# Sixteen more fulfilled semaphore instructions in ScalarE's stream, behind its first small loads

## The chip, the cores and the metric

The kernel runs on one core of a Trainium2 chip. The metric is the device time of one execution in microseconds (us); lower is better. The core has five engines with a queue of instructions each: TensorE (PE, whose weight loads are shown as PEld), VectorE (DVE), ScalarE (ACT), GpSimd (POOL) and SyncE (SP). They run on their own and wait for each other through semaphores, which are counters: a producer adds to one when it is done, and a consumer waits until it has reached a value.

## The reference

The kernel mixes a state-space branch and a dense branch with a gate. The input `x` has 2048 rows (time steps) of 640 columns, in bf16.

```python
x = A_x
g = _sigmoid((x * gate_w).sum(-1, keepdims=True))
# a: complex diagonal state-space model
dt = jnp.exp(log_dt)
Lam_bar = jnp.exp(dt * Lam)
B_bar = ((Lam_bar - 1.0) / Lam)[:, None] * Bmat
Bu = jnp.einsum("bld,pd->blp", x + 0j, B_bar)
for t in range(L):
    h = Lam_bar[None, :] * h + Bu[:, t, :]
y = 2.0 * jnp.einsum("blp,dp->bld", hseq, Cmat).real + x * Dskip[None, None, :]
# b: gelu MLP, hidden width 1728
h = jnp.einsum("bsd,df->bsf", x, w1) + b1
h = _gelu(h)
b = jnp.einsum("bsf,fd->bsd", h, w2) + b2
return g * a + (1 - g) * b
```

## The kernel before, in words

The 2048 time steps are cut into four quarters of 512 (`q`), and the recurrence into eight blocks of 256 (`ssm(b)`). For each quarter TensorE does five kinds of work: the hidden layer of the dense branch (`m1`, x times w1, L653 for its first eight column groups and L675 for the rest), the input projection of the state-space branch (`bproj`, L718), the second layer (`mains` in `outsT` and the like, L1013 and L807), the output projection (L1083, L920), and small tails. Each group of matmuls fills one of eight PSUM banks, and ScalarE empties it: gelu for `m1` (L662 for the first eight groups, L682 for the rest), a copy for `bproj` (L727). VectorE computes tables from the small vectors once, and then multiplies, scans and combines.

The order on each engine is not written out by hand. Each operation is added with `op(name, eng, dur, reads, writes, fn, prio)`. A planner (`Sched.order`) runs through time and takes, on each engine, the operation with the lowest `prio` number among those whose predecessors are finished by its own estimates. What then comes out is one fixed stream for each engine. `Emitter.wait` (its `wait_ge` stands on L139) writes the waits ahead of an operation, one for each semaphore that the engine has not yet waited for to that value. The build step then places such waits on instructions: a wait either sits on the instruction itself or on an EVENT_SEMAPHORE instruction of its own in the same queue.

The start of the kernel is where the change lies:

- GpSimd sets the tile `rows` to zero (`rz`, L386) and increments `pool_s`, the first value of that semaphore.
- ScalarE issues six DMAs: one piece of w1 (`w1load(0, "act", -110, reads=["rz"])`), which waits for `rz`, and then the small vectors into rows of `rows`: b1b (priority -101), `lre`, `lim`, `ldt` and `b1a` (-100 to -97).
- TensorE warms up (L416), transposes pieces of x (L428), and starts the hidden layer (L653). In between it transposes `rows` (L455), and VectorE copies the result to `cols` (L460, operation `cols1`).
- ScalarE takes the exponential of a part of `cols` (`dt`, L465), and VectorE and ScalarE in turn make angles (L470, L471, L485 to L493), a magnitude (`amag`, L478) and two sines (L498, L499), from which VectorE makes the tables of the state-space branch.
- Then ScalarE does the gelus of the first eight groups (L662), in the order of the banks 0 to 7. The ninth group of matmuls, the first of L675, takes bank 0 over again and so waits for the first gelu.

Exp, Sin and gelu need different function tables in ScalarE. The build step puts an ACT_TABLE_LOAD into ScalarE's stream wherever the next function is not in the table that is loaded; there are three, shown with the lines 465, 498 and 662 of the operations that need them.

The first operations of that chain are

```python
        def f_dt():
            return inc("act", nc.scalar.activation(dtb[:, :], lcol[:, 2, :], ACT.Exp))

        op("dt", "act", 0.3, ["lcol"], ["dtb"], f_dt, prio=-950)
```

`lcol` is a part of `cols`. The number -950 puts `dt` ahead of everything else on ScalarE as soon as `cols` is there in the planner's time, and not before.

Of the kernel before, what the change touches and what calls it, by code (L numbers as in the profile page):

```python
# [147 lines left out]
class Prog:  # L148
# [8 lines left out]
    def op(self, name, eng, dur, reads, writes, fn, prio=None, lat=0.0, after=()):  # L157
        deps = {}
        for k in reads:
            for w in self.last_w.get(k, ()):  # L160
                deps[w.idx] = w
        for k in writes:
            for w in self.last_w.get(k, ()):
                deps[w.idx] = w
            for r in self.last_r.get(k, ()):
                deps[r.idx] = r
        for a in after:
            deps[a.idx] = a
        deps = list(deps.values())
        E = self.E  # L170

        def run(eg, deps=deps, eng=eng, fn=fn):
            E.wait(eng, *[d.done for d in deps if not (eng == "pe" and d.eng == "pe")])
            return fn()

        it = self.sch.add(name, eng, dur, deps, run, prio=prio, lat=lat)
        for k in writes:
            self.last_w[k] = [it]
            self.last_r[k] = []
        for k in reads:  # L180
            self.last_r.setdefault(k, []).append(it)
        return it


def bass_gated_mix__ssm_conv_s5__dense_activation_gelu__prompt_kernel(
# [18 lines left out]
    _, S, D = A_x.shape  # L204
# [21 lines left out]
    with ExitStack() as es:  # L226
# [69 lines left out]
        sems = {}  # L296
# [11 lines left out]
        op = pr.op  # L308
# [108 lines left out]
            return inc("pe", t)  # L417

        op("warm", "pe", 2.7, (), [("bank", 4)], f_warm, prio=-1000)

        for i, (k, c0, c1) in enumerate(((0, 0, 2), (1, 0, 2), (0, 2, 4), (1, 2, 4))):
            bank = (7, 6, 7, 6)[i]
# [777 lines left out]
```

## Time and profile before

| What | us |
|---|---|
| median of the three runs | 212.67 (212.52 to 212.89) |
| profiled execution, first to last instruction (span) | 211.0 |
| difference, time around the span | 1.6 to 1.7 |
| PE busy | 207.5 (98%) |
| DVE busy | 191.1 (91%) |
| ACT busy | 102.7 (49%) |
| POOL busy | 4.2 (2%) |

The profile is of one execution, and of that it gives the span; the time around it is what the median of the other runs has beyond the span. Busy times leave out instructions that only wait or issue. The mean granted clock of TensorE is 1.000 over the span. An engine's share of the span is a mean over stages; what counts at a place in time is who waits for whom there. The profile has these views: the chain that ended last, followed back from the last instruction; a timeline of instructions, with the idle time before each and what ended it; and, for a source line, all instructions of that line, semaphore instructions among them, which the timeline leaves out. Times in all views are counted from the first instruction. Names such as "ACTq" or "PEldq" mean the queue of that engine.

### The profile page before, as it was taken

To read this page: it belongs to the slowest core of one execution; us is meant where nothing else is said; L and a number is where in the kernel's file an instruction comes from. 1 tells how busy PE (TensorE), PEld (TensorE's weight loads), DVE (VectorE), ACT (ScalarE), POOL (GpSimd) and SP (SyncE) were. 2 spreads that over 40 slices of the span, in tenths; PEclk is the share of its full clock that TensorE was granted. 3 is DMA by queue.
4 is the path that set the end of the run, shared out by engine and by line. 5 is a ranking of instruction groups with operands and counts; after the bars stand their busy time and mean duration, and the time that the engine had idled before them with its cause. 6 is when DMAs were issued, how large, how long until landed. Compare 5 with 4: busy or idle time off the path is not lost.

```text
span 211.0 us, 2539 instructions
## 1 busy us (share of the span) xinstructions
PE 207.5 (98%) x987; PEld 95.7 (45%) x1004; DVE 191.1 (91%) x244; ACT 102.7 (49%) x166; POOL 4.2 (2%) x12
## 2 busy tenths in 40 slices
PE   8999999999999999999999999999999999999996
PEld 4544444444444444444444444444444444444444
DVE  2399999999999999999999999899999999899482
ACT  2399556678950523556674222456665243304321
POOL 1000000030000000000010000000010000000000
DMA  6999999999800020043464000005622000006623
GB/s 190 259 221 118 203 173 216 381 203 175 184 2 4 0 50 0 0 95 67 90 57 117 0 3 0 0 2 116 150 59 100 0 0 4 0 0 141 134 76 99
DMA packets 50247, 19.47 MB, mean 92 GB/s; under 512 B 43068, under 2 KB 48828, under 8 KB 50236
## 3 DMA queue, kind: packets, MB, share of 16 engines
q1 hardware_dynamic: 47904, 17.59, 39.5%
q0 software_dynamic: 1600, 1.32, 4.2%
q10 hardware_dynamic: 732, 0.40, 0.8%
q8 instruction: 8, 0.13, 0.3%
q14 instruction: 3, 0.02, 0.1%
HBM read 8.68 MB, written 2.63 MB: 54 GB/s over the span
## 4 chain that ended last, share of the span: by engine, by line
PE 98%; issue 0%; DVE 0%
PE ps L675 22%; PE ps L718 20%; PE ps L1013 20%; PE ps L1083 15%; PE ps L807 5%; PE ps L653 4%; PE ps L920 4%; PE ps L827 1%; PE ps L416 1%; PE ps L696 1%; PE ps L880 1%; PE ps L1048 1%; PE ps L428 0%; PE ps L844 0%; DVE W1sb L952 0%
## 5 line engine op out<-in xcount | busy, mean ns | idle before, releaser
L675 PE MATMUL ps<-xT,W1sb 128*128 128x512 bf16 x214 | 47.5, 379 | 0.3
L760 DVE TENSOR_TENSOR_SCAN W<-atab,V 128x1280 bf16<-128x1280 f32 x16 | 44.3, 2811 | 0.3
L718 PE MATMUL ps<-xT,BT 128*128 128x512 bf16 x196 | 43.3, 379 | 0.2
L1013 PE MATMUL ps<-Gl,W2sb 128*128 128x512 bf16 x192 | 42.8, 379 | 0.2
L682 ACT ACTIVATE Gl<-ps,cols 128x512 bf16<-128x512 f32 x44 | 29.9, 695 | 15.5 <-PE ps L675 15.5
L675 PEld LDWEIGHTS ps<-xT,W1sb 128*128 128x128 bf16 x220 | 21.5, 98 | 26.0
L1083 PE MATMUL ps<-Hb,CT 128*128 128x512 bf16 x150 | 32.9, 379 | 0.0
L727 ACT ACTIVATE U<-ps 128x512 bf16<-128x512 f32 x40 | 23.6, 596 | 14.7 <-PE ps L718 14.7
L718 PEld LDWEIGHTS ps<-xT,BT 128*128 128x128 bf16 x200 | 19.5, 98 | 23.8 <-ACT Gt L704 0.4
L1013 PEld LDWEIGHTS ps<-Gl,W2sb 128*128 128x128 bf16 x195 | 18.9, 98 | 23.3 <-issue 0.7
L1083 PEld LDWEIGHTS ps<-Hb,CT 128*128 128x128 bf16 x150 | 14.7, 98 | 17.7
L1021 ACT ACTIVATE E1T<-ps,cols 128x512 bf16<-128x512 f32 x15 | 10.0, 687 | 26.2 <-PE ps L1013 14.7
L1091 ACT ACTIVATE E2T<-ps 128x512 bf16<-128x512 f32 x15 | 9.0, 597 | 21.7 <-PE ps L1083 21.7
L627 DVE SCALAR_TENSOR_TENSOR trf<-xn,gwb 128x640 bf16<-128x640 bf16 x16 | 13.2, 823 | 0.4
L505 DVE TENSOR_TENSOR Hb<-Hb,V 128x1280 bf16<-128x1280 bf16 x16 | 12.5, 822 | 0.3
L505 DVE TENSOR_TENSOR V<-V,W 128x1280 bf16<-128x1280 bf16 x16 | 12.5, 821 | 0.3
L505 DVE TENSOR_TENSOR V<-mr,U 128x2560 bf16<-128x2560 bf16 x8 | 11.9, 1492 | 0.3
L505 DVE TENSOR_TENSOR Hb<-c,W 128x2560 bf16<-128x2560 bf16 x8 | 11.9, 1490 | 0.2
L807 PE MATMUL ps<-W2sb,Gl 128*128 128x512 bf16 x51 | 11.8, 379 | 0.1
L505 DVE TENSOR_TENSOR W<-mi,U 128x2560 bf16<-128x2560 bf16 x8 | 11.9, 1484 | 0.0
L505 DVE TENSOR_TENSOR V<-s,W 128x2560 bf16<-128x2560 bf16 x8 | 11.9, 1484 | 0.0
L1071 ACT ACTIVATE xT<-xT,cols 128x512 bf16<-128x512 bf16 x15 | 10.0, 713 | 0.9 <-DMA cols<-in_A_Dskip_dram 0.9
(103 smaller groups left out, 149.4 us busy)
## 6 DMA issues: line engine op xcount, KB each, us to landing
W2sb<-in_B_w_dram SPq DMA_DIRECT2D x1, 2080.0 KB, 8.7
out_dram<-xn SPq DMA_DIRECT2D x3, 640.0 KB, 5.7
xn<-in_A_x_dram POOLq DMA_DIRECT2D x2, 640.0 KB, 6.9
W1sb<-in_B_w_dram SPq DMA_DIRECT2D x4, 256.0 KB, 4.0
trf<-grow SPq DMA_DIRECT2D x4, 256.0 KB, 4.8
xn<-in_A_x_dram SPq DMA_DIRECT2D x1, 640.0 KB, 7.6
W1sb<-in_B_w_dram SPq DMA_DIRECT2D x1, 480.0 KB, 6.1
W1sb<-in_B_w_dram SPq DMA_DIRECT2D x1, 400.0 KB, 6.9
```

Source lines behind the costliest of these rows:

```text
L505: return inc("dve", nc.vector.tensor_tensor(out=o, in0=a, in1=b, op=o_))
L627: t = inc("dve", nc.vector.scalar_tensor_tensor(out=scr[:, :], in0=xn[q % 2][:, c, :], scalar=1.0, in1=gwb[:, :], op0=ALU.mult, op1=ALU.mu ...
L675: t = nc.tensor.matmul(PS[bank][:, :], W1sb[:, k, jf * 128:(jf + 1) * 128], xT[q][:, k, :], start=(k == 0), stop=(k == KD - 1))
L682: return inc("act", nc.scalar.activation(Gl[q % 2][:, jf, :], PS[bank][:, :], ACT.Gelu_apprx_tanh, bias=b1col[:, jf:jf + 1]))
L718: t = nc.tensor.matmul(PS[bank][:, :], BT[:, ci, kd, k * 128:(k + 1) * 128], xT[q][:, kd, :], start=(kd == 0), stop=(kd == KD - 1))
L727: return inc("act", nc.scalar.activation(dst, src, ACT.Copy, scale=1.0 if ci == 0 else -1.0))
L760: t = inc("dve", nc.vector.tensor_tensor_scan(out=g[:, ci, :], data0=a, data1=v[:, ci, :], initial=0.0, op0=ALU.mult, op1=ALU.add))
L807: t = nc.tensor.matmul(PS[bank][:, :], Gl[q % 2][:, jf, t4 * 128:(t4 + 1) * 128], W2sb[:, jf, 0:DN], start=False, stop=False, skip_group_c ...
L1013: t = nc.tensor.matmul(PS[bank][:, :], W2sb[:, jf, d * 128:(d + 1) * 128], Gl[q % 2][:, jf, :], start=(jf == 0 and not lead), stop=(jf == ...
L1021: return inc("act", nc.scalar.activation(E1T[:, d, :], PS[bank][:, :], ACT.Identity, bias=cols2[:, 0, d:d + 1]))
L1071: return inc("act", nc.scalar.activation(xT[q][:, d, :], xT[q][:, d, :], ACT.Copy, scale=cols2[:, 1, d:d + 1]))
L1083: t = nc.tensor.matmul(PS[bank][:, :].rearrange("p (s t) -> p s t", s=2), CT[:, ci, k, d * 128:(d + 1) * 128], Hb[:, 2 * (q % 2):2 * (q % ...
```

## The change

An operation `pad` is added for ScalarE. It has 32 calls of `wait_ge` on `pool_s` for the value 1, reads `rz` and writes nothing. Its priority is -96.

```diff
         op("warm", "pe", 2.7, (), [("bank", 4)], f_warm, prio=-1000)
 
+        def f_pad():
+            for _ in range(32):
+                nc.scalar.wait_ge(sems["pool_s"], 1)
+
+        op("pad", "act", 0.1, ["rz"], [], f_pad, prio=-96)
+
         for i, (k, c0, c1) in enumerate(((0, 0, 2), (1, 0, 2), (0, 2, 4), (1, 2, 4))):
```

In the built program this gives sixteen more semaphore instructions on ScalarE. What they ask of `pool_s` was already fulfilled when ScalarE's first DMA was issued.

## The prediction

> **What bounds the kernel now.** I read the chain of waits that ended last first, then the timeline of ScalarE around the place of the change, then the semaphore records there.
>
> ```profile
> PE 98%; issue 0%; DVE 0%
> ```
>
> TensorE is the chain for 98% of the span: whatever costs time must open a gap on PE. The chain cut to 12 to 20 us shows how PE passes from the first hidden-layer matmuls (L653, eight banks filled in turn) to the next ones (L675, which take the banks over again):
>
> ```profile
> 11.81 2.16 PE ps L653 x10
> 13.97 5.40 PE ps L675 x25
> ```
>
> There is no gap at that seam, and the chain nowhere passes through ACT. The timeline of ScalarE from 3 to 21 us is the view that decides here:
>
> ```profile
> 3.64 0.40 ACTq L333 DMA_DIRECT2D rows<-in_B_b_dram  x1
> 4.07 1.28 ACT L465 ACT_TABLE_LOAD   x1 [4.07 <-issue]
> 8.62 0.21 ACT L465 ACTIVATE dtb<-cols 128x5 bf16<-128x5 f32 x1 [3.27 <-DVE cols L460]
> 9.14 0.21 ACT L478 ACTIVATE amag<-acol 128x5 f32<-128x5 f32 x1 [0.31 <-DVE thcol L471]
> 9.36 1.28 ACT L498 ACT_TABLE_LOAD   x1
> 10.72 0.34 ACT L498 ACTIVATE trf<-trf 128x165 f32<-128x165 f32 x1
> 10.96 0.32 ACT L499 ACTIVATE trf<-trf 128x165 f32<-128x165 f32 x1
> 11.31 1.28 ACT L662 ACT_TABLE_LOAD   x1
> 12.60 4.74 ACT L662 ACTIVATE Gl<-ps,cols 128x512 bf16<-128x512 f32 x8
> ```
>
> Columns: start, duration, engine and line. ScalarE issues its last small load until 4.04, loads the table for Exp at once (4.07 to 5.35), and then waits 3.27 us for `cols` from VectorE (L460, ends at 8.59). The load of the table thus lies wholly inside a wait. From 8.62 on nothing is idle: Exp, Exp, a second table, two Sin, a third table, and at 12.60 the first gelu, which ends at 13.29 and frees the first bank.
>
> The last view is PE's own semaphore records between 13.2 and 13.5 us (L139 is the line of every wait):
>
> ```profile
> L139 PEldq EVENT_SEMAPHORE  x1: 51/51/51, 13.3 to 13.3; - x1
> ```
>
> By the trace's records it starts 0.04 us after the first gelu ends: TensorE's queue is already waiting for ScalarE there, and only work queued ahead (to 13.81, where the first L675 matmul starts) hides it. So ScalarE's chain from 8.62 is a second critical path, with a small slack.
>
> **That slack.** Gelu ends 13.29; +0.04 to the semaphore record; +0.05 for it; +0 to 0.10 until the weight load starts (the record that ends at 2.01 has one 0.003 us behind it; 0.10 is an assumed upper end); +0.005 to 0.054 from weight load to matmul (the rows at 3.98 and at 8.14). An unhindered start is 13.385 to 13.535, the real one 13.81: slack 0.28 to 0.42 us. I take 0.33.
>
> **The change, part by part.** Nothing is removed. `f_pad` asks 32 times for a value of `pool_s` that the w1 load at 0.97 has already waited for.
>
> *Place.* Priority -96 puts it behind the last of the small loads (-97) and ahead of the Exp of L465, which needs `cols`. Its planned 0.1 us ends long before the planner has `cols` ready, so no other engine's order should move, and it adds no increment and no DMA.
>
> *How waits become instructions.* The records show one wait on an ACTIVATE and up to two on a semaphore record ahead of it: the five waits in front of L455 are one on the transpose and two records with two each (7.2 to 7.4 us). They also show which goes where: the wait written first sits on the instruction itself (`l_lre` at L455), and the one written last stays on the semaphore record next to it. For L465 that makes 32 + 1 = 33 waits: one on the ACTIVATE, 32 on sixteen records. This is the sixteen of the title. But the wait on `cols` is the one written last, so it goes from the ACTIVATE to the sixteenth record, and a fulfilled one takes its place.
>
> *The sixteen as such.* No row shows such records back to back on ScalarE. One there lasts 17 ns; with pauses, two on SP (L1169) start 58 ns apart, two on PE (64.6 us) 111 ns. Fifteen cost 0.26 us (15 x 17 ns) to 1.7 us (15 x 111), by the SP rows 0.87. They run from 4.04 to at most 5.7, and 8.59 is when `cols` comes: hidden by VectorE's lateness on either bound, cost 0. Without that cover it would be 0.9 us.
>
> *What is queued behind the sixteenth.* It now holds ScalarE's queue until 8.59, and everything behind it: the first ACT_TABLE_LOAD, if that stands between the records and the ACTIVATE. The trace has no case of a table load with semaphore records ahead. The three loads there are each directly ahead of the ACTIVATE that needs the new function (L465, L498, L662), none earlier, though the Exp table could have been loaded before the DMA issues at 0.97. So I take it that the load stays right in front of its ACTIVATE, behind the records.
>
> The Trainium skill, "ScalarE: Activation LUTs", section "Step-by-step: what each stage is for", says the same: the compiler places the ACT_TABLE_LOAD right before the ACTIVATE that needs it.
>
> *Price.* `cols` ends 8.59; +0.03 until the sixteenth record (as at 159.4 us, where one follows an ACTIVATE's end by 31 ns); +0.017 to 0.028 for it; +0.03 to 0.045 to the next instruction; +1.283 for the load; +0.01 to the ACTIVATE (11.31 + 1.28 = 12.59, gelu at 12.60). Exp starts at 9.97 instead of 8.62: **ScalarE is 1.36 us late** (1.34 to 1.39). Every link behind it hands this on whole: dtb to acol on VectorE within 0.04 us, thcol to amag, amag directly to the second load, and the five VectorE operations that the Sin awaits start from thcol too. The first gelu ends at 14.65.
>
> *Sum.* 1.36 - 0.33 = **1.03 us** of gap on PE (0.92 to 1.11 from the bounds above). After that it is not repeated: ScalarE does a gelu each 0.57 us where PE takes 1.08 us per bank, so it is back in step at some 20 us, and the other banks have 0.8 us or more in hand where only 0.33 is still missing. VectorE's tables come 1.36 us later too, 0.33 relative to PE; by the trace's update times PE's first matmuls on its results (L1083, weight load at 72.09) have 3.6 us in hand, the last at least 3.3. The end of the kernel moves with PE.
>
> This is made against the profiled span of 211.0 us, which becomes 212.0. What lies around it (212.67 - 211.0 = 1.6 to 1.7) I leave as it is: 212.67 + 1.03 = **213.7 us**. About 0.2% is what a measurement of this kernel can tell from no change; 1.03 is 0.48%.
>
> **A rule that speaks for more.** In the trace each of the second and third loads has its ACTIVATE behind it with no pause beyond the wait for data (load ends 12.59, gelu 12.60).
>
> The Trainium skill, "ScalarE: Activation LUTs", section "What ACT_TABLE_LOAD costs", gives 1283 ns for the load, as the trace has, but adds a drain of about 1380 ns to each switch, which these rows do not show. By it the sum would be about 2.4 us, an estimate.
>
> **The rivals.**
>
> *Cover kept (not slower).* If the table load is put ahead of the sixteen records, or the wait on `cols` stays on the ACTIVATE, the load still runs inside the idle 4.04 to 8.59. The records and the load together need 0.87 + 1.28 = 2.15 of 4.55 us. What is left is the extra record after `cols`: on VectorE at 196.1 us an operation with such a record in between starts 0.10 us after the one before it ends, against 0.03 to 0.04 without, so 0.06 us. It decides at the slack: a ScalarE delay below 0.28 costs nothing. Time 212.67. For it: nothing in the trace proves where a load goes when records stand ahead. Against: each load seen sits directly at its ACTIVATE. That the waits are merged away and the change does nothing gives the same time.
>
> *All sixteen behind the release.* If the record with `cols` came first, fifteen more (0.87) and the load (1.28) would follow 8.59: 2.23 - 0.33 = 1.9 us, 214.6. Against: the order of waits at L455 and the fulfilled waits being written earlier.
>
> *A cold clock.* The 256-column matmuls of L653 are 213 ns apart until 5.5 us and 109 ns from 5.9: PE ran at half speed for its first 4.9 us. If the gap of 1.03 us brought that back for as long, half of 4.9 us would be added: 1.03 + 2.45, so 216.1. Against: the view has no PE gap of that length to judge by, and 1 us is short against 4.9.
>
> *A pause behind the moved load*, as the rule above has it. Behind the first load lie 3.27 us of waiting now, which would hide a pause of any length up to that; moved into the chain, the load would show it. From rows it is between 0 (the 0.01 us behind the third load) and 3.27; with one more load's length (1.28) the time would be 215.0. Against: the 0.01.
>
> **How the numbers follow.** Main case 0.76 (213.4 to 214.1, from 0.92 to 1.11 widened by 0.2 for the scatter of the runs, 212.52 to 212.89, and for the restart of PE). Cover kept or nothing done 0.16, of which 0.02 falls outside 0.2% on the fast side. All sixteen behind 0.03, cold clock 0.04, pause 0.01. Slower: 0.76 + 0.03 + 0.04 + 0.01 = 0.84; same 0.14; faster 0.02, as PE has no idle time for ScalarE to give back. The main case alone leaves out more than 2 in 10, so the range reaches down to the kept cover: 212.5 to 214.1.
>
> **What would show it.** In ScalarE's timeline the load of L465 moves from 4.07 to some 8.7, the Exp to 9.97, the first gelu to 13.96; in the chain of waits ScalarE's L465 to L662 appear between VectorE's `cols` and PE's L675, which starts at 14.8 instead of 13.81. Sixteen ScalarE semaphore records appear, fifteen from 4.1 to 5.0, the last at 8.6. The forecast is wrong if the load is still at 4.07 to 5.0, if PE starts L675 less than 0.9 us later, or if L653 or L675 pitches change.

## The result, and the profile after

| | before | with the change |
|---|---|---|
| median of 13 runs, us | 212.64 (212.25 to 213.15) | 213.26 (212.79 to 213.72) |
| ratio, with 95% interval | 1 | 1.0031 (1.0023 to 1.0040) |
| span of the profiled run, us | 211.0 | 212.0 |

The change costs 0.62 us in the medians. The span of the two profiled runs grows by 1.0 us. Those two numbers do not agree, and the larger part of the experiments goes to that difference.

The line numbers of the changed kernel are six higher behind L418: L465 is now L471, L653 is L659, L662 is L668, L675 is L681. The timeline of ScalarE, from 3.6 us:

```profile
3.63 0.40 ACTq L333 DMA_DIRECT2D rows<-in_B_b_dram  x1
8.71 1.28 ACT L471 ACT_TABLE_LOAD   x1 [8.71 <-DVE cols L466]
10.01 0.21 ACT L471 ACTIVATE dtb<-cols 128x5 bf16<-128x5 f32 x1
10.52 0.21 ACT L484 ACTIVATE amag<-acol 128x5 f32<-128x5 f32 x1 [0.31 <-DVE thcol L477]
10.75 1.28 ACT L504 ACT_TABLE_LOAD   x1
...
12.69 1.28 ACT L668 ACT_TABLE_LOAD   x1
13.99 4.74 ACT L668 ACTIVATE Gl<-ps,cols 128x512 bf16<-128x512 f32 x8
```

The bracket shows it: the idle time before the first table load is now ended by VectorE's `cols`. Before, that load ran at 4.07 and the ACTIVATE carried this bracket. Exp starts at 10.01 instead of 8.62, the first gelu at 13.99 instead of 12.60.

The records of the added waits themselves, by their line (shortest, median and longest in ns, then the first and last start in us):

```profile
L423 ACTq EVENT_SEMAPHORE  x15: 38/38/38, 4.1 to 5.2; - x15
```

Fifteen lie between 4.1 and 5.2 us, in the idle time. The sixteenth has the line of the ordinary waits, since it was the wait on `cols` to begin with, and is seen in the chain of waits from 8 to 24 us:

```profile
8.42 0.20 DVE cols L466
8.62 0.02 issue
8.64 0.04 ACTq L139
8.68 0.03 issue
8.71 1.28 ACT L471
...
13.99 0.70 ACT Gl L668
14.68 0.14 issue
14.82 5.56 PE ps L681 x25
```

The chain leaves TensorE here, goes through `cols`, the record, the moved table load and on to the gelu, and comes back to TensorE at 14.82, 1.01 us later than before. In TensorE's timeline the gap has its releaser:

```profile
14.82 5.56 PE L681 MATMUL ps<-xT,W1sb 128*128 128x512 bf16 x25 [0.82 <-ACT Gl L668]
```

The bracket counts from the end of the matmul before, whose record lasts 0.38 us although the next one usually starts 0.216 us behind its start. By the starts (13.62 and 14.82) TensorE loses 0.99 us here.

Behind that place the first matmul of each line stands 1.01 us later than in the profile of before, up to the end (L718 at 20.21 instead of 19.20, the last such, L880, at 200.65 instead of 199.64). TensorE thus loses its time at this one seam and loses nothing more behind it.

### The profile page after: what moved, and what is told of

Same layout as the page of the kernel before. It is cut to its first block, busy times and chain, and to the rows that moved or that the text cites. A ratio compares the mean times of both kernels' runs of the same rounds, so it can differ in the third digit from the quotient of the medians.

```text
span 212.0 us, 2555 instructions
## 1 busy us (share of the span) xinstructions
PE 207.6 (98%) x987; PEld 95.4 (45%) x1004; DVE 191.0 (90%) x244; ACT 102.7 (48%) x166; POOL 4.2 (2%) x12
## 3 DMA queue, kind: packets, MB, share of 16 engines
q0 software_dynamic: 1600, 1.32, 4.7%
## 4 chain that ended last, share of the span: by engine, by line
PE 95%; ACT 2%; DVE 1%; issue 1%; ACTq 0%
PE ps L681 22%; PE ps L724 20%; PE ps L1019 20%; PE ps L1089 15%; PE ps L813 5%; PE ps L926 4%; PE ps L659 2%; PE ps L833 1%; PE ps L416 1%; PE ps L702 1%; PE ps L886 1%; PE ps L1054 1%; ACT L668 1%; ACT L471 1%; PE ps L434 0%
## 5 line engine op out<-in xcount | busy, mean ns | idle before, releaser
L681 PE MATMUL ps<-xT,W1sb 128*128 128x512 bf16 x214 | 47.5, 379 | 1.1 <-ACT Gl L668 0.8
L681 PEld LDWEIGHTS ps<-xT,W1sb 128*128 128x128 bf16 x220 | 21.4, 98 | 27.0 <-issue 1.3
```

The lines of the kernel that those rows point to most:

```text
L681: t = nc.tensor.matmul(PS[bank][:, :], W1sb[:, k, jf * 128:(jf + 1) * 128], xT[q][:, k, :], start=(k == 0), stop=(k == KD - 1))
```

## Experiments

All times around the span below are the mean, over all runs of a kernel, of the run's time less its span. For before it was 1.62 us in each of the groups of runs (1.61 to 1.63), for the change 1.33. Each ratio is to the kernel before as it ran alongside in the same group; the spans of before in the group of the result are not on record, apart from the profiled one. The diffs of experiments 1, 2, 3, 8 and 12 are against the change, the others against the kernel before; `...` marks lines left out. Line numbers move a little with each edit; the seam is always the first gelu and the matmuls that wait for it.

**1. The same waits, with the wait on cols written first.**

```diff
-        op("pad", "act", 0.1, ["rz"], [], f_pad, prio=-96)
+        op("pad", "act", 0.0, ["lcol"], [], f_pad, prio=-951)
```

The operation, with its 32 waits as they were, now stands behind `cols1` in the program, just ahead of `dt`.

> The same 32 extra waits and the same sixteen semaphore records at the same place in ScalarE's stream, but the wait on cols is written ahead of them, so that it sits on the ACTIVATE of dtb again and all sixteen records are fulfilled at once. If what costs is the wait on cols that went in front of the first table load: records from 4.1 to 5.3 us, load 5.3 to 6.6, Exp of dtb at 8.62 as before, time within 0.2% of before (212.6). If the sixteen records themselves cost: 213.2 to 213.3 as with the change.

Measured 212.22 us, ratio 0.9978 (0.9966 to 0.9989). ScalarE's timeline:

```profile
5.30 1.28 ACT L471 ACT_TABLE_LOAD   x1 [5.30 <-issue]
8.12 0.21 ACT L471 ACTIVATE dtb<-cols 128x5 bf16<-128x5 f32 x1 [1.54 <-DVE cols L460]
```

The sixteen records only push the load from 4.07 to 5.30, and the ACTIVATE carries the wait again (`cols` itself came 0.5 us earlier in this execution). TensorE has no gap at the seam: its row there has no bracket.

```profile
13.37 4.91 PE L681 MATMUL ps<-xT,W1sb 128*128 128x512 bf16 x22
```

So the order in which two waits are written decides over 1 us, and the records cost nothing there. But the kernel was faster than before by more than its interval, which neither theory had.

**2. One extra wait instead of 32.**

```diff
-            for _ in range(32):
+            for _ in range(1):
```

> One extra wait instead of 32: one semaphore record, which holds the wait on cols, with the table load behind it. If the moved wait costs: load at 8.7, Exp of dtb at 9.99, TensorE's gap at the seam 0.97 us in the profile, time 213.2, the same as with 32. If the number of records costs: a sixteenth of 0.62 us, so 212.7, not to be told from before.

Measured 213.55 us, ratio 1.0039 (1.0024 to 1.0053), with the load at 8.48 behind `cols` and this on TensorE:

```profile
14.59 3.61 PE L681 MATMUL ps<-xT,W1sb 128*128 128x512 bf16 x16 [0.73 <-ACT Gl L668]
```

One record does the same harm as sixteen, as the theory of the moved load has it. By the starts of the matmuls the gap is 0.90 us, where 0.97 was expected. The expected time of 213.2 was missed, though: the span is on average 212.03 as with the change (212.02), and the time around is 1.45, not 1.33; the rest is within the scatter of six runs.

**3. The 32 waits, with a one-column Exp ahead of them.**

```diff
+        pre = SB("pre", [128, 1], BF16)
+
+        def f_pre():
+            return inc("act", nc.scalar.activation(pre[:, :], one, ACT.Exp))
+
+        op("pre", "act", 0.0, ["rz"], ["pre"], f_pre, prio=-96.5)
```

> The 32 waits as in the change, and ahead of them a one-column Exp on a constant into a scratch tile that nothing reads (added work), so that the table load comes before the records. If the load is what costs: load at 4.07, records behind it, Exp of dtb at 8.66 to 8.72 (0.06 to 0.1 late, inside the slack of 0.28 to 0.42), time within 0.2% of before (212.6). If the records cost, or the wait being on a record does: 213.2.

Measured 212.19 us, ratio 0.9981 (0.9972 to 0.9989). The load stands at 4.06, and TensorE has no gap:

```profile
4.06 1.28 ACT L424 ACT_TABLE_LOAD   x1 [4.06 <-issue]
8.53 0.21 ACT L478 ACTIVATE dtb<-cols 128x5 bf16<-128x5 f32 x1 [2.97 <-DVE cols L473]
```

```profile
13.64 4.70 PE L688 MATMUL ps<-xT,W1sb 128*128 128x512 bf16 x21
```

Exp of dtb starts 0.11 us after `cols` ends (8.42), 0.08 later than in before, which the slack hides. So the wait may stay on the record: what costs is the load behind it. Again the kernel was faster than before, with a time around the span of 1.34.

**4. The kernel before, once more.** No edit.

> The kernel before, unchanged, for the spread of its executions: ratio 1.000. The change moved the profiled spans by 1.0 us and the medians by only 0.62. If TensorE in a usual execution of before loses some 0.3 to 0.4 us between the cols transposition (8.1 us) and its first matmul of the second group (13.81 in the first profile), which the late gelu then covers, a profile of another execution shows that matmul at 14.0 to 14.3 and a gap of 0.2 to 0.5 us ahead of it with a DMA as releaser. If the first profile is usual in this, it is at 13.8 again and the spans differ elsewhere.

Measured 212.76 us, ratio 1.0004 (0.9993 to 1.0014). The first matmul of L675 stands at 14.20 us here, which the expectation had taken for a sign of late DMAs. It is not one: there is no gap ahead of it, `cols` is late by the same 0.39 us, and so is everything from 6.7 us on. What differs is when TensorE comes to full speed (last section). The guess that usual executions of before lose 0.4 us behind `cols` thus fell. The runs on record had the answer: time less span is 1.63 here, as in all runs of before, and 1.33 with the change, with next to no spread (0.03).

So the question became what shortens the time around the span, and whether it is the place or the number of the records.

**5. Sixteen records in the last quarter.**

```diff
             m2_out(cs[1])
+
+            def f_pad():
+                for _ in range(32):
+                    nc.scalar.wait_ge(sems["pool_s"], 1)
+
+            op("pad", "act", 0.0, [], [], f_pad, prio=-1, after=[e1op[cs[1]]])
             cproj(cs[0])
```

> Sixteen fulfilled records on ScalarE as in the change, but in the last quarter (after its second evacuation of dense results, near 196 us), where ScalarE idles; the start of the kernel is that of before. In the runs so far the time around the span was 1.62 us for before, 1.45 with one more instruction on ScalarE, 1.33 to 1.34 with sixteen or seventeen more. If the number of instructions in ScalarE's stream sets it: span 211.0 as before, around 1.33, time 212.3. If it is the place at the start (records in front of the first table load or Exp): around 1.62, time 212.6.

Measured 212.33 us, ratio 0.9991 (0.9977 to 1.0004); mean span 210.99 against 210.95 of before, time around 1.33 against 1.62. The ratio alone says little, since the spans scatter by 0.3 us; the time around, which scatters by 0.03, is clear. At the start or in the last quarter, the records shorten it alike.

**6. Four in the same place** (`range(8)`).

> The same with four more instructions on ScalarE. If the number in the stream sets the time around the span and it falls with each one until some boundary: between 1.33 and 1.45. If only the first counts: 1.45. If the place counts: 1.62. Span 211.0 in each case.

Measured 212.54 us, ratio 1.0006 (0.9995 to 1.0018). The time around is 1.48, but not steadily: from 1.33 to 1.60 from run to run.

**7. Seventeen on GpSimd.**

```diff
+        def f_pad():
+            for _ in range(32):
+                nc.gpsimd.wait_ge(sems["pool_s"], 1)
+
+        op("pad", "pool", 0.0, ["iota"], [], f_pad, prio=-59)
```

> Seventeen more fulfilled records on GpSimd behind its iotas, where it waits 41.9 us for w2 anyway; ScalarE as before. If the time around the span hangs on ScalarE's stream alone: 1.62 and 212.6. If more instructions on any engine, or a larger program, shorten it: 1.33 and 212.3.

Measured 212.65 us, ratio 1.0002 (0.9989 to 1.0014), time around 1.62. So it hangs on ScalarE's stream and not on GpSimd's; the other three engines were not tried.

**8. The lateness without the moved load.** As in 3 the load is ahead; then 36 waits, the one on `cols` placed so that it sits on the first of eighteen records.

```diff
...
-            for _ in range(32):
-                nc.scalar.wait_ge(sems["pool_s"], 1)
+            for i in range(36):
+                nc.scalar.wait_ge(*((sems["dve_s"], 8) if i == 19 else (sems["pool_s"], 1)))
```

> The table load ahead (by a one-column Exp on a constant into scratch, added work), then eighteen records of which the first holds the wait on cols and seventeen follow it, at 77 ns each as the change's profile shows: Exp of dtb 1.31 to 1.36 us late without any moved load. If only ScalarE's lateness counts, whatever makes it: gap on TensorE at the seam of 0.95 to 1.05 us, span 212.0, with around 1.33 a time of 213.3. If the load as such disturbs more than by its length: span nearer 211.0.

Measured 213.35 us, ratio 1.0040 (1.0021 to 1.0058); mean span 212.06, time around 1.34. Exp starts at 9.99, as late as with the change. TensorE's timeline:

```profile
14.80 3.40 PE L688 MATMUL ps<-xT,W1sb 128*128 128x512 bf16 x15 [0.85 <-ACT Gl L675]
```

The gap is that of the change (0.82; by the starts 1.01 and 0.99), made by records alone. Here they cost 77 ns each, because they stand behind `cols`; in the change the same records are free.

**9 and 10. 128 and 144 more.** Three records ahead of each of the 40 evacuations of the input projection, and 8 or 24 in the last quarter as in 5.

```diff
                     def f_ev(k=k, ci=ci, bank=bank):
...
+                        for _ in range(6):
+                            nc.scalar.wait_ge(sems["pool_s"], 1)
                         return inc("act", nc.scalar.activation(dst, src, ACT.Copy, scale=1.0 if ci == 0 else -1.0))
```

> ScalarE's stream longer by 128 fulfilled records: three ahead of each of its 40 evacuations of the input projection (0.23 us in waits of 0.48) and eight in the last quarter. ScalarE fetches its instructions in pieces of 8192 bytes, which at 64 bytes each would be 128 of them (an estimate from the records: its fetches at 45.1 us in before and at 187 to 189 us with sixteen more lie about 128 instructions apart). If the time around the span depends on where the last such border falls, it comes round again: around 1.62, time 212.6. If a longer stream is simply better: 1.33 or less. Span 211.0 in both cases.

> The same with 144 more, sixteen past a whole piece. Border: around 1.33, a last ScalarE fetch inside the span near its end, time 212.3. Longer is better: 1.33 or less as with 128. If with 128 it is 1.33 too, the border falls.

Measured 212.57 us with 128, ratio 0.9999 (0.9984 to 1.0014), time around 1.62; and 212.40 with 144, ratio 0.9995 (0.9979 to 1.0011), time around 1.32. So a longer stream is not simply better: 128 more give the time around of before, and sixteen beyond that give the change's. That fits a border in the stream every 128 instructions. The times alone would also fit a shorter period that divides 128, since no count between 19 and 128 was tried; the fetches (see experiment 11) speak for 128.

**11. Eight in the last quarter** (`range(16)`).

> Eight more on ScalarE in the last quarter. With four more the time around varied from 1.33 to 1.60 and a fetch came 1.3 us after the span's end. If the border decides, with eight that fetch moves to the span's end or into it and the time around settles at 1.33 to 1.40. If it is only noise in what four do: 1.45 to 1.5, spread as wide.

Measured 212.40 us, ratio 0.9990 (0.9974 to 1.0005), time around 1.33 and steady again.

The instruction fetches go with it. On the page, the row of the queue that fetches in pieces of 8192 bytes, for the kernel before and then for the change:

```profile
q14 instruction: 3, 0.02, 0.1%
```

```profile
q14 instruction: 4, 0.03, 0.1%
```

The columns are packets, MB and share. The trace's records give the time of the added one: 188.6 us with the change, 195.6 with sixteen late, 209.6 with eight late, 212.3 with four late, which is 1.3 us after that span's end; with none or one more there is none up to the end of the records. The number of fetches alone decides nothing, for 128 more have four too:

```profile
q14 instruction: 4, 0.03, 0.1%
```

There the added fetch lies at 96.0 us, and none lies near the end. Counted in ScalarE's instructions its place is nearly fixed. In every trace that has this fetch, 186 to 193 of them had started when it began, and the next one, with 144 more, came at 319. The kernels with the long time around end at 183 or 311 instructions, short of such a fetch; those with the short one at 191 to 202 or 327, behind it; 184 (one more) and 187 (four more) lie between.

**12. The change with 112 more**, 128 in all: three ahead of each such evacuation of the first three quarters and 22 in the last.

```diff
+                        for _ in range(6 if q < 3 else 0):
+                            nc.scalar.wait_ge(sems["pool_s"], 1)
...
+                for _ in range(44):
+                    nc.scalar.wait_ge(sems["pool_s"], 1)
```

> The change as it is, and 112 further fulfilled records where ScalarE waits anyway (three ahead of each input-projection evacuation of the first three quarters, 22 in the last quarter), 128 more than before in all, so that ScalarE's stream ends at the same place of a fetch piece as in before. If the change is the sum of two terms, +1.03 in the span from the moved table load and -0.29 around it from the border, only the first is left: span 212.0, around 1.62, median 213.6 to 213.7, ratio 1.005. If the load's loss was really 0.6: 213.2.

Measured 213.70 us, ratio 1.0041 (1.0029 to 1.0053); mean span 212.01, time around 1.63. With the end of the stream where it was in before, the time around is back and TensorE's gap stays (0.82 by the bracket). The time is the forecast's 213.7, against 212.75 of before in this group: 0.95 us in the medians and 0.85 between the mean spans (211.16 for before), which is the moved load alone within the scatter. The other way round, kernels 1 and 3 are the change without its loss: at 212.2 both beat the kernel before, and 0.28 to 0.29 us of their 0.4 come from the time around the span, the rest is within the scatter of spans.

## Why the prediction was right, and where it was off

The forecast was 213.7 us and slower; it is 213.26 and slower. The direction and the mechanism inside the span were right, and one term was missing. For that reason 213.26 lies below the range of the main case itself (213.4 to 214.1). It lies in the stated range only because that was drawn down to 212.5 for another case, the kept cover, which did not happen: that part was luck.

- *How waits become instructions.* As forecast: fifteen records of fulfilled waits, the sixteenth with the wait on `cols`, a fulfilled wait on the ACTIVATE. Experiments 1 and 2 show that this exchange is what matters.
- *The sixteen as such, 0.87 us, hidden.* Hidden, as experiment 1 shows. They cost 77 ns each, not 58, so 1.12 us from 4.07 to 5.19, inside the bounds of 0.26 to 1.7.
- *The load behind the records.* The step that was argued and not seen before is shown: load at 8.71. The Trainium skill's sentence on it ("ScalarE: Activation LUTs", "Step-by-step: what each stage is for") holds in this case.
- *ScalarE 1.36 us late.* 1.38 by the starts of Exp, of which 0.02 is a later `cols`; the first gelu is 1.385 late, so every link handed it on. The rows of the forecast add up to 1.34 to 1.37, not to 1.39. The sixteenth record took 38 ns where 17 to 28 stood in the sum.
- *Slack 0.33.* From the end of the gelu (14.67) to TensorE's restart (14.82) are 0.145 us; 13.81 - 13.29 - 0.145 gives 0.375 in the profile of before. The term was 0.045 too small, inside its bounds.
- *Sum 1.03 us.* 1.01 at the seam of the two profiles, and 0.9 to 1.1 between the mean spans (212.02 against 210.95 to 211.16 in the groups of before).
- *"What lies around it (212.67 - 211.0 = 1.6 to 1.7) I leave as it is."* This step failed. It became 1.33: -0.29 us. With it the sum is 1.03 - 0.29 = 0.74, against 0.62 in the medians and 0.7 in the means. The forecast treated the time outside the span as the same for every program; sixteen more instructions on ScalarE moved it. It goes with where ScalarE's stream ends between two fetches.
- *Nothing for ScalarE to give back.* Inside the span that held. The gain lay outside it, so the chance for "faster", in the case of a kept cover, was too low: kernels 1 and 3 are that case, and their times are 0.2% below before.
- *Rivals.* Cover kept: no, the load stands at 8.71. All sixteen behind the release: not so, but experiment 8 puts eighteen records there, without the load, and gets 77 ns a record. Cold clock: no, the matmuls behind the gap of 1 us are 215 ns apart, those ahead of it 216. A pause behind the moved load: no, the Exp starts 0.01 us after its end.

What stays open is what ScalarE does in those 0.29 us. Nothing in the records lies behind a span's end but the fetch at 212.3 with four late. That a fetch behind the last instructions holds up the end in the kernel before is an argument; no trace of that kernel has such a fetch. Shown is that the time around follows the number of ScalarE's instructions, with 0, 8, 16, 128 and 144 more, and not GpSimd's. That the border of a fetch is its cause is inferred from the counts. With one and with four more the time around lies between the two values, and why is not resolved. Taking records out of ScalarE's stream was not tried.

## What to carry to other kernels

An extra wait, even one long fulfilled, can push another wait off its instruction and in front of a table load that used to run inside that wait; look at which instruction carries which wait, and write first the wait that is fulfilled last. Take times from spans and from whole runs apart: eight more instructions on one engine moved what lies around the span by 0.3 us here, so a difference of 0.1 to 0.2% between two kernels is not yet a matter of their work. When a change costs less than its own term, look for a second term with the other sign before doubting the first.

## What the runs showed of the hardware that was not expected

The spans of one and the same kernel scatter by 0.9 us (before, 210.6 to 211.5 in one group of 27 runs), and in the first six profiles they go with the moment at which TensorE comes to full speed. The matmuls of 256 columns go over from 213 to 109 ns apart at 5.85 us in the first profile of before, 6.7 in the second, 5.7 with the change, 5.45 in experiment 3, and about 4.0 in experiments 1 and 2. The spans of the four without a late gelu follow in the same order: 210.6 us (experiment 1), 210.9 (experiment 3), 211.0 and 211.4 (before). Six profiles are no proof that nothing else adds to the scatter. The mean clock of 1.000 in the profile does not show it, but the timeline does. TensorE before, first profile, and then experiment 1, at the same three matmuls:

```profile
3.99 0.82 PE L653 MATMUL ps<-xT,W1sb 128*128 128x256 bf16 x3
```

```profile
4.03 0.49 PE L659 MATMUL ps<-xT,W1sb 128*128 128x256 bf16 x3
```

The same work takes 0.82 us in the one and 0.49 in the other. The Trainium skill, "TensorE: Matmul & The Clock Gate", section "What's actually happening", has full speed after some 3.4 us of sustained work, watched in a free-running window, so that the moment varies by 500 ns either way. The moment wanders here too, but by more: from TensorE's first matmul at 0.78 it took 3.2 to 5.9 us.

The other surprise is the time around the span: 1.62 us or 1.33, depending on the number of instructions in ScalarE's stream. The Trainium skill, "Runtime: NRT & Kernel Launch", section "Instruction fetch mechanics", calls the cost of crossing a block's border mostly hidden and gives blocks of 16 KiB; the fetches here are of 8192 bytes on this queue (16384 on the other). At none of the fetches inside the span does the chain of before show TensorE pausing for more than 0.05 us, and the kernels that have one near the end are 0.29 us shorter around the span.
